# An attention and MLP kernel ordered anew: planner costs and deadlines refitted, four more blocks of exponentials on VectorE, one gelu over w1, U doubled

## The chip, the cores and the metric

The kernel runs on one core of a Trainium2 chip. The metric is the device time of one execution in microseconds (us). "Before" and "changed" are compared on the same chip in the same rounds; only in the first comparison were three of the four runs of "before" taken earlier, before the prediction. A ratio here is the mean time of one kernel's fast runs over that of the other's fast runs in those rounds, with a 95% interval; it is not quite the ratio of the medians that are quoted. All times quoted are of fast runs; one run of the kernel before, of 1394.7 us, was a slow outlier (granted TensorE clock 0.562, against 0.986 to 0.993 in the other runs of its set) and is in no ratio.

## The reference

```python
x = A_x                                         # 2048 tokens, width 640, bf16
xn = layernorm(x)
s = attention(xn, A_wqkv, A_wo)                 # 32 heads of 20, softmax over 2048 keys
g = silu(B(xn))                                 # B below
return x + s * g

def B(x):                                       # shifts(.) moves quarters of the columns by -2..2 tokens
    h  = gelu(layernorm(x) @ w1)
    x1 = x + shifts(h) @ w2
    return x1 + gelu(layernorm(x1) @ w3) @ w4
```

The softmax alone has 32 x 2048 x 2048 exponentials. ScalarE makes most of them, and they fill 789.5 of the 913.2 us of the profile before.

## The kernel before

The program writes a list of tasks, each for one engine with an assumed duration. A planner in the kernel simulates the engines when the program is built and fixes the order of every engine's queue from that simulation. That order then stands: an instruction whose semaphore is not there yet holds up everything behind it in its queue. (In the run `flat_offsets` below, ScalarE waited 8.5 us for value products that stood behind 140 background matmuls on PE.)

Exponentials are made in two ways. On ScalarE one activation takes a 128x1024 score tile (two PSUM banks, two heads). In a "block unit" (`score_both`) the scores of all four heads of a key tile are computed at once: two heads go to ScalarE and two to VectorE, which converts them to 16-bit integers in `U` (L1401) and scales them four times into `SS` (L1308). The scaled bits, read as bf16, are pieces whose weighted sum on PE approximates the exponential. `ND` says how many such blocks each group of queries has. A block covers two key tiles and spares ScalarE two activations.

```python
SYNC_LAT = 130.0                       # one latency for every engine pair, ns
def c_dve(n, kind="psum"):             # assumed VectorE durations
    if kind == "psum" or kind == "1x": return 185 + 1.042 * n
    if kind == "4x":                   return 185 + 0.2605 * n
...
self.LAG = 3;  self.AHEAD = 4          # one lag for all of VectorE's block work
self.ND = ([1,2,3,3], [3,3,3,3], ..., [3,3,3,3], [3,3,2,1])     # 90 blocks
...
pl.pool("W", 3); pl.pool("S", 2)       # banks 5..7 for background, 2 pairs for scores, bank 4 for values
...
# score_both: two heads to S for ScalarE, two to a pair of W banks for VectorE
T("pe", 220, fn, ..., acq=[("S", hs), ("W", h0, h1)])
slot = self.exp_act(hs, sa)            # ScalarE
T("dve", c_dve(1024), fnu, ..., due=cfg.T0 + (self.nact + cfg.LAG) * cfg.STEP)
```

Everything else (projections, both MLP layers, the output projection) is background work for PE and VectorE, placed between scores. It uses the three W banks, which block units use as well.

Of the kernel before, what the change touches and what calls it, by code (L numbers as in the profile page):

```python
# [86 lines left out]
SYNC_LAT = 130.0  # L87
# [40 lines left out]
class Planner:  # L128
    def __init__(self):
# [19 lines left out]
        self.mode_cost = 100.0  # L149
        self.reserve = 0.0  # L150

    def pool(self, name, nslots):
        self.pools[name] = nslots

# [115 lines left out]

    def schedule(self, verbose=False):
# [13 lines left out]
        for t in reversed(tasks):  # L285
            d = t.due if t.due is not None else INF
            for (sid, sync) in t.succs:
                s = tasks[sid]
                sd = s.prio - s.dur - (SYNC_LAT if sync else 0.0) - t.lat
                if sd < d:  # L290
                    d = sd
            if d == INF:
                d = horizon + 1e6
            t.prio = d
# [24 lines left out]
        while done < n:  # L319
            best = None  # L320
            for e in ENGINES:
# [6 lines left out]
                early = None  # L328
                k = 0
                saved = set()  # L330
                while h and k < WINDOW:
# [5 lines left out]
                    if t.acq:  # L337
# [3 lines left out]
                        short = None  # L341
                        for a in t.acq:
                            ft = sorted(x[0] for x in pstate[a[0]])[len(a) - 2]
                            if ft > rt:
                                rt = ft
                            if len(a) > 2 and ft > tf:
                                short = a[0]
                        if short is not None and rt < INF and r0 <= tf + self.reserve:
                            saved.add(short)
# [31 lines left out]
            for pname, *handles in t.acq:  # L381
                ps = pstate[pname]
                idle = [i for i in range(len(ps)) if ps[i][0] <= st + 1e-9]
                mid = (len(ps) - 1) / 2
                if len(handles) == 2:
                    pick = min(((i, j) for i in idle for j in idle if i < j), key=lambda x: (x[1] - x[0], ps[x[0]][0] + ps[x[1]][0]))
                elif pname == "W":
                    pick = (max(idle, key=lambda i: (abs(i - mid), -ps[i][0])),)
                else:
                    pick = (min(idle, key=lambda i: ps[i][0]),)  # L390
                for si, handle in zip(pick, handles):
                    ft, rel_tid = ps[si]
                    handle.slot = si
                    held[id(handle)] = (pname, si)
                    ps[si] = (INF, None)
                    if rel_tid is not None:
                        t.preds.add(rel_tid)
                        tasks[rel_tid].succs.append((t.id, True))
# [14 lines left out]
            for rh in (t.rel if isinstance(t.rel, (list, tuple)) else () if t.rel is None else (t.rel,)):  # L413
                pname, si = held.pop(id(rh))
                pstate[pname][si] = (t.finish + t.lat + SYNC_LAT, t.id)
            for (sid, sync) in t.succs:
# [3 lines left out]
                rt = t.finish + t.lat + (SYNC_LAT if sync else 0.0)  # L420
# [164 lines left out]
class Cfg:  # L585
# [5 lines left out]
    def __init__(self, S=2048, D=640, H=32, F=1536):  # L591
# [12 lines left out]
        self.STEP = 960.0  # L604
        self.BLK = [(2, 3), (6, 7), (10, 11), (14, 15)]
        self.LAG = 3
        self.AHEAD = 4
        self.UNITS = ((), ((3, 0, 1),), ((0, 0, 2), (2, 1, 2)), ((0, 0, 2), (2, 1, 2), (6, 0, 1)),
                      ((0, 0, 2), (1, 1, 2), (4, 0, 2), (5, 1, 2)))
        self.HPS = 6  # L610
        self.EARLY = 15570.0
        self.WO = 20580.0
        self.B1 = (0.64, 0.7)
        self.B2 = (3.06, 0.95)
        self.LEAD = 65220.0
        self.LEAD0 = 56120.0
        self.VLEAD = 9440.0
        self.ND = (
            [1, 2, 3, 3],
            [3, 3, 3, 3],  # L620
            [3, 3, 3, 3],
            [3, 3, 3, 3],
            [3, 3, 3, 3],
            [3, 3, 3, 3],
            [3, 3, 3, 3],
            [3, 3, 2, 1])
# [28 lines left out]
def c_dve(n, kind="psum"):  # L655
    if kind == "psum" or kind == "1x":
        return 185 + 1.042 * n
    if kind == "2x":
        return 185 + 0.521 * n
    if kind == "4x":  # L660
        return 185 + 0.2605 * n
    if kind == "recip":
        return 150 + 6.25 * n
# [3 lines left out]
def c_act(n):  # L667
    return 90 + 0.8333 * n


def c_pe(ninstr, N):
    return ninstr * max(29.0, 0.107 * N)
# [9 lines left out]
class Gen:  # L682
# [50 lines left out]
    def wbank(self, h, dtype=FP32):  # L733
        return self.bank(self.W0 + h.slot, dtype)
# [19 lines left out]
    def build(self, plan_only=False):  # L754
        nc, pl = self.nc, self.pl
        with contextlib.ExitStack() as es:
# [8 lines left out]
            self.W0 = 5  # L765
            pl.pool("W", 3)
            pl.pool("S", 2)
# [14 lines left out]
    def program(self):  # L782
# [15 lines left out]
        for quad in range(cfg.NQUAD):  # L798
# [3 lines left out]
            if quad + 1 < cfg.NQUAD:  # L802
                self.fetch(quad + 1)
            if quad == 1:
                self.v_load(1)
                self.v_proj(1)
            self.run_b(quad)
# [3 lines left out]
        self.T("sp", 10, None, reads=self.out_atoms, name="join", due=cfg.T0 + self.nact * cfg.STEP + 8000.0)  # L811
# [8 lines left out]
    def setup_consts(self):  # L820
# [20 lines left out]
        T("dve", 200, lambda e: e.tensor_reduce(eaug[:, :], e4[:, :], axis=AX.X, op=ALU.add),  # L841
          reads=[A("e4")], writes=[A("eaug")], name="eaug")
        maskh = self.maskh = self.alloc("maskh", [1], FP32)
        T("dve", 200, lambda e: e.tensor_reduce(maskh[:, :], maskn[:, :], axis=AX.X, op=ALU.add), reads=[A("maskn")], writes=[A("maskh")],
          name="maskh0")
        T("dve", 200, lambda e: e.tensor_scalar(maskh[:, :], maskh[:, :], 0.0, None, op0=ALU.is_lt),
# [12 lines left out]
    def alloc_persistent(self):  # L859
# [15 lines left out]
        T("dve", 100, lambda e: e.tensor_tensor(self.maskq[:, :], self.maskh[:, :], self.eaug[:, :], op=ALU.add),  # L875
          reads=[A("maskh"), A("eaug")], writes=[A("maskq")], name="maskq")
        T("dve", 100, lambda e: e.tensor_scalar(self.qbias[:, :], self.eaug[:, :], cfg.OFFSET / cfg.scale, None, op0=ALU.mult),
# [4 lines left out]
        self.U = self.alloc("U", [4096], U16)  # L882
        self.SS = self.alloc("SS", [4, 4096], U16)
# [13 lines left out]
        self.PVB = 4  # L897
# [883 lines left out]
```

## Time and profile before

The first median was 915.4 us (3 runs); together with the run measured beside the changed kernel it is 913.87 us (4 runs).

The profiled run took 914.91 us and its span, from the first to the last instruction, is 913.2 us. ScalarE is the engine to account for: span = its busy time + its idle time. The prediction below works this account out. Two lines of ScalarE's order in time that it does not show matter later. They give start, duration, instruction and, in brackets, the idle time before it and who ended it:

```profile
23.22 2.55 ACT L986 ACTIVATE arena<-arena 128x640 bf16<-128x640 bf16 x3 [5.12 <-DVE arena L982]
...
39.54 21.45 ACT L1369 ACTIVATE arena<-psum 128x1024 bf16<-128x1024 f32 x23 [0.48 <-PE psum L1327]
```

The first is an activation of the opening layer norm that waited 5.1 us for a small VectorE result. The second is the first exponential.

### The profile page before, as it was taken

To read this page: it belongs to the slowest core of one execution; us is meant where nothing else is said; L and a number is where in the kernel's file an instruction comes from. 1 tells how busy PE (TensorE), PEld (TensorE's weight loads), DVE (VectorE), ACT (ScalarE), POOL (GpSimd) and SP (SyncE) were. 2 spreads that over 40 slices of the span, in tenths; PEclk is the share of its full clock that TensorE was granted. 3 is DMA by queue.
4 is the path that set the end of the run, shared out by engine and by line. 5 is a ranking of instruction groups with operands and counts; after the bars stand their busy time and mean duration, and the time that the engine had idled before them with its cause. 6 is when DMAs were issued, how large, how long until landed. Compare 5 with 4: busy or idle time off the path is not lost.

```text
span 913.2 us, 34227 instructions
## 1 busy us (share of the span) xinstructions
PE 838.0 (92%) x15654; PEld 367.2 (40%) x15654; DVE 714.5 (78%) x999; ACT 863.2 (95%) x911; POOL 37.8 (4%) x69
## 2 busy tenths in 40 slices
PE   3899999999999999999998999999997999889996
PEld 1434333444334334433333545433443535324453
DVE  7657788888898889977878778777887667768855
ACT  5898999999999999999999999899999989999995
POOL 7300000000000000100000000000000000100000
PEclk9999999999999999999999999999999999999998
DMA  7003221020122003122123212321122020311322
GB/s 234 11 8 102 77 53 39 25 73 21 36 82 64 19 19 88 31 60 57 43 52 94 72 42 63 89 66 47 45 68 74 18 73 24 99 48 37 108 68 74
DMA packets 83548, 54.81 MB, mean 60 GB/s; under 512 B 52556, under 2 KB 77340, under 8 KB 83276
## 3 DMA queue, kind: packets, MB, share of 16 engines
q1 hardware_dynamic: 83404, 52.62, 20.6%
q8 instruction: 123, 2.02, 0.9%
q14 instruction: 21, 0.17, 0.1%
HBM read 37.91 MB, written 10.63 MB: 53 GB/s over the span
## 4 chain that ended last, share of the span: by engine, by line
ACT 56%; PE 34%; DVE 6%; DMA 3%; issue 1%; SPq 0%; ACTq 0%
ACT arena L1369 51%; PE psum L747 13%; PE psum L1345 11%; PE psum L1286 4%; PE psum L1327 3%; PE psum L1319 2%; DMA arena<-recips 2%; DVE arena L1401 2%; ACT arena L1723 1%; ACT arena L1670 1%; DMA recips<-arena 1%; DVE arena L1308 1%; ACT arena L986 1%; DMA arena<-in_A_x_dram 1%; ACT arena L1739 1%
## 5 line engine op out<-in xcount | busy, mean ns | idle before, releaser
L1369 ACT ACTIVATE arena<-psum 128x1024 bf16<-128x1024 f32 x844 | 789.5, 1034 | 25.4 <-PE psum L1327 16.1
L1345 PE MATMUL psum<-arena 128*32 128x512 bf16 x5088 | 388.7, 382 | 19.3 <-ACT arena L1369 15.1
L747 PE MATMUL psum<-arena 128*32 128x320 bf16 (+1 forms) x5952 | 360.7, 335 | 12.3 <-DVE arena L1124 5.3
L1401 DVE TENSOR_SCALAR arena<-psum 128x1024 uint16<-128x1024 f32 x177 | 216.1, 1221 | 83.3 <-PE psum L1327 82.0
L1308 DVE TENSOR_SCALAR arena<-arena 128x2048 uint16<-128x2048 uint16 (+1 forms) x240 | 219.2, 956 | 2.2 <-PE psum L1319 1.7
L747 PEld LDWEIGHTS psum<-arena 128*32 128x32 bf16 x5952 | 153.3, 97 | 153.5 <-issue 21.6
L1345 PEld LDWEIGHTS psum<-arena 128*32 128x32 bf16 x5088 | 108.5, 95 | 162.6 <-ACT arena L1369 125.6
L1286 PE MATMUL psum<-arena 128*22 128x512 bf16 x1688 | 163.7, 381 | 1.7 <-ACT arena L1369 1.4
L1319 PE MATMUL psum<-arena 128*22 128x512 bf16 x1440 | 115.0, 380 | 2.6 <-DVE arena L1308 2.5
L1327 PE MATMUL psum<-arena 32*128 32x512 bf16 x776 | 82.0, 387 | 14.1 <-DVE arena L1401 5.7
L1286 PEld LDWEIGHTS psum<-arena 128*22 128x22 bf16 x1688 | 43.1, 92 | 58.1 <-issue 13.4
L1327 PEld LDWEIGHTS psum<-arena 32*128 32x128 bf16 x776 | 20.9, 91 | 92.6 <-ACT arena L1369 59.0
L1319 PEld LDWEIGHTS psum<-arena 128*22 128x22 bf16 x1440 | 35.2, 92 | 43.1 <-DVE arena L1308 6.8
L1719 DVE CAST arena<-psum 128x512 bf16<-128x512 f32 x48 | 32.9, 687 | 7.7 <-PE psum L747 7.4
L1170 DVE CAST arena<-psum 128x512 bf16<-128x512 f32 x40 | 27.3, 687 | 9.1 <-PE psum L747 9.0
L1523 DVE SCALAR_TENSOR_TENSOR arena<-psum,arena 128x320 bf16<-128x320 f32 x32 | 15.6, 488 | 17.7 <-PE psum L747 17.2
L1452 DVE TENSOR_TENSOR arena<-arena 128x512 bf16<-128x512 f32 x28 | 19.2, 685 | 9.6 <-DMA arena<-recips 9.6
L935 DVE BATCH_NORM_STATS2 arena<-arena 128x6 f32<-128x320 bf16 x52 | 23.8, 482 | 3.5 <-DMA arena<-in_A_x_dram 3.5
L1734 DVE TENSOR_TENSOR arena<-psum,arena 128x320 bf16<-128x320 f32 x32 | 15.6, 487 | 13.1 <-PE psum L747 12.8
L1034 PE MATMUL psum<-arena 128*32 128x128 bf16 x320 | 8.5, 243 | 16.3 <-DVE arena L949 14.8
L1231 DVE CAST arena<-psum 128x320 bf16<-128x320 f32 x32 | 15.4, 487 | 9.8 <-PE psum L747 9.4
L1723 ACT ACTIVATE arena<-arena 128x12288 bf16<-128x12288 bf16 x2 | 20.9, 10446 | 0.0
(102 smaller groups left out, 295.1 us busy)
## 6 DMA issues: line engine op xcount, KB each, us to landing
arena<-in_B_w_dram SPq DMA_DIRECT2D x48, 160.0 KB, 2.5
arena<-recips SPq DMA_DIRECT2D x28, 256.0 KB
arena<-arena SPq DMA_DIRECT2D x124, 32.0 KB, 1.8
arena<-in_B_w_dram SPq DMA_DIRECT2D x4, 960.0 KB, 5.5
arena<-in_A_x_dram SPq DMA_DIRECT2D x8, 320.0 KB, 5.4
arena<-in_A_x_dram SPq DMA_DIRECT2D x16, 160.0 KB, 3.0
out_dram<-arena SPq DMA_DIRECT2D x16, 160.0 KB, 1.8
arena<-keys SPq DMA_DIRECT2D x28, 80.0 KB
```

The source lines that it names most:

```text
L747: ins = e.matmul(pb[32 * c:32 * c + 32, 0:N], lhsT(k, c), rhs(k, c), start=(k == 0), stop=(stop and k == nk - 1), tile_position=(0, 32 * c))
L935: lambda e, li=li, n=n, hh=hh: e.bn_stats(st[:, li, 6 * hh:6 * hh + 6], xn[:, n, hD * hh:hD * hh + hD]),
L1170: T("dve", c_dve(512), lambda e, h=h, c=c: e.tensor_copy(KS[:, 512 * c:512 * c + 512], self.wbank(h)[:, 0:512]), reads=[wa], writes=[A("KS ...
L1286: ins = e.matmul(pb[32 * i:32 * i + 22, 0:512], VA[:, ql, kts[i // 2], i, :], PT[:, slots[i // 2][0].slot, 512 * (i % 2):512 * (i % 2) + 512],
L1308: T("dve", c_dve(w, "4x"), lambda e, v=v, dst=dst: e.tensor_scalar(dst, U[:, 0:w], 0.5, EXP_B[v], op0=ALU.mult, op1=ALU.add), reads=halves ...
L1319: ins = e.matmul(pb[32 * i:32 * i + 22, 0:512], wv, dst[:, at:at + 512].bitcast(BF16), start=first, stop=final, tile_position=(0, 32 * i))
L1327: return e.matmul(out, self.KT[32 * i:32 * i + 32, b, 128 * kt:128 * kt + 128], self.QT[32 * i:32 * i + 32, b, 512 * qc:512 * qc + 512], s ...
L1345: ins = e.matmul(out[32 * c:32 * c + 32, :], self.KT[:, b, 128 * kt + 32 * c:128 * kt + 32 * c + 32], self.QM[:, gb, 2 * a + jj, :], start ...
L1369: lambda e: e.activation(self.PT[:, hp.slot, :], self.psum[:, 1024 * hs.slot:1024 * hs.slot + 1024], AF.Exp, scale=cfg.scale),
L1401: return e.tensor_scalar(dst, self.psum[:, 512 * (self.W0 + lo):512 * (self.W0 + hi + 1)], a_exp, EXP_BIAS, op0=ALU.mult, op1=ALU.add)
L1719: T("dve", c_dve(512), lambda e, h=h, fc=fc, i=i: e.tensor_copy(GT[:, i, fc, :], self.wbank(h)[:, 0:512]), reads=[wa], writes=at, name=f"g ...
L1723: T("act", 2600 + c_act(2 * FC * 512), lambda e: e.activation(GT[:, :, :, :], GT[:, :, :, :], AF.Gelu_apprx_tanh), reads=gta, writes=gta, ...
```

## The change

What it is meant to do, as the diff reads: give the planner the durations and latencies as measured on the chip, so that its order holds there; refit all deadlines on it; use the room that VectorE then has. The core of the diff, shortened (`...` marks what is left out):

```diff
-SYNC_LAT = 130.0
+SYNC_LAT = {"pe": 225.0, "act": 158.0, "dve": 136.0, "pool": 160.0, "sp": 60.0}
 def c_dve(n, kind="psum"):
-        return 185 + 1.042 * n            # and 185 + 0.2605 * n for "4x"
+        return 72 + 1.042 * n             # and  68 + 0.2605 * n
 def c_act(n):
-    return 90 + 0.8333 * n
+    return 68 + 0.8333 * n
...
-        self.LAG = 3                      # with LEAD, LEAD0, VLEAD, EARLY, WO, B1, B2
-        self.AHEAD = 4
+        self.DUE = dict(k0=-37.9, k1=-9.1, ..., u0=4.0, s0=28.5, u1=7.6, s1=12.5, u2=39.8, s2=57.4,
+            u3=-14.3, s3=3.0, u4=34.6, s4=0.5, u5=59.4, s5=-9.6, u6=-9.6, s6=31.8, u7=-13.7, s7=18.1)
+        self.SAVE = 1; self.THIRD = False; self.FALL = False; self.AHEAD = 3
-            [1, 2, 3, 3], ... [3, 3, 2, 1])
+            [2, 2, 3, 3], ... [3, 3, 3, 4], [3, 3, 3, 3], [3, 3, 4, 3], [4, 2, 3, 2])
...
-            pl.pool("W", 3); pl.pool("S", 2)
+            pl.pool("B", 7)               # "SD": a score pair and a pair of W banks, taken as one
+            pl.kind("SD", "B", [(r + q, x + y) for r, x in pairs for q, y in high])
+            if self.cfg.SAVE: pl.saves = {"SD": "W"}     # hold W tiles back when an SD is short
...
-        self.U = self.alloc("U", [4096], U16);  self.SS = self.alloc("SS", [4, 4096], U16)
+        self.U = self.alloc("U", [2, 4096], U16);  self.SS = self.alloc("SS", [3, 4096], U16)
...
-        self.hx = self.alloc("hx", [2, KC, 512], BF16)      # gelu over w1 in two halves
+        self.hx = self.alloc("hx", [4, KC, 512], BF16)      # one gelu over all of it
-          name=f"u{quad}_{qc}_{kt}", due=cfg.T0 + (self.nact + cfg.LAG) * cfg.STEP)
+          name=f"u{quad}_{qc}_{kt}", due=self.at(self.nact, f"u{quad}"))
```

Offsets in `DUE` are counted in ScalarE steps of 0.96 us. `u0` to `u7` and `s0` to `s7` shift the deadlines of the conversions and scalings of one quad (four heads). Also changed, and not shown here: durations that were written as plain numbers (small VectorE operations are planned at 90 ns in place of 100 to 260), the places of the blocks within a group of queries (`UNITS`), and the priority of VectorE's drain of the value bank, which now goes before background work.

## The prediction

> **What bounds the kernel now.** I read the share of busy time first, then the granted clock (0.992 over the span, so no throttled state), then the chain that ended last, then every wait of ScalarE, then ScalarE's instructions in order of time, and last what PE and VectorE did around the long waits.
>
> ```profile
> PE 838.0 (92%) x15654; PEld 367.2 (40%) x15654; DVE 714.5 (78%) x999; ACT 863.2 (95%) x911; POOL 37.8 (4%) x69
> ...
> ACT 56%; PE 34%; DVE 6%; DMA 3%; issue 1%; SPq 0%; ACTq 0%
> ...
> L1369 ACT ACTIVATE arena<-psum 128x1024 bf16<-128x1024 f32 x844 | 789.5, 1034 | 25.4 <-PE psum L1327 16.1
> ```
>
> ScalarE is busy 863.2 of 913.2 us and heads the chain. Nearly all of it is 844 exponentials, 789.5 / 844 = 0.935 us each back to back. PE shows 92%, but its ends are modelled and it also waits for ScalarE 353 times before column scores (125.6 us at its weight loads), so much of that is pacing by ScalarE. The span is therefore ScalarE's busy time plus its 50.0 us of idle. Where the idle is, ScalarE's waits tell:
>
> ```profile
> ACT arena L1369 <- PE psum L1327: 16.1, 15, 3.5
> ACT arena L1369 <- PE psum L1286: 5.4, 2, 4.1
> ACT arena L986 <- DVE arena L982: 5.1, 1, 5.1
> ACT arena L966 <- DMA arena<-in_A_x_dram: 3.0, 2, 1.7
> ACT arena L1369 <- PE psum L1345: 2.8, 7, 0.8
> ```
>
> The three L1369 rows are the listed waits of the exponentials (24.3 of the 25.4 us that the group shows). The last exponential ends at 902.5 us, so 913.2 - 902.5 = 10.7 us is the tail. The rest, 50.0 - 25.4 - 10.7 = 13.9 us, is start-up before the first exponential at 39.5 us. L1327 is the row-tiled score of a block unit: it makes one tile for ScalarE and one for VectorE, and needs banks from the pool that projections and the MLP also use. Around the longest such wait (start, duration, instruction, idle before it) the timeline has:
>
> ```profile
> 577.53 1.49 DVE L1742 SCALAR_TENSOR_TENSOR arena<-arena 128x1280 bf16<-128x1280 bf16 x1 [1.09 <-ACT arena L1739]
> ...
> 579.34 0.69 DVE L1308 TENSOR_SCALAR arena<-arena 128x2048 uint16<-128x2048 uint16 x1
> 579.48 1.48 PEld L747 LDWEIGHTS psum<-arena 128*32 128x32 bf16 x48 [1.14 <-DVE arena L1734]
> ...
> 580.06 1.22 DVE L1401 TENSOR_SCALAR arena<-psum 128x1024 uint16<-128x1024 f32 x1
> ...
> 581.44 0.40 PE L1327 MATMUL psum<-arena 32*128 32x512 bf16 x4
> ...
> 581.89 1.02 ACT L1369 ACTIVATE arena<-psum 128x1024 bf16<-128x1024 f32 x1 [3.48 <-PE psum L1327]
> ```
>
> VectorE was waiting in order for a tanh; then it drained a background bank, PE used that release for 48 background matmuls, the VectorE score tile was drained only at 581.3, and only then could the next score pair start. Nothing was saturated: the order of the queues was bad. The 4.06 us wait at 77.4 us has the same form: 28 background matmuls stood on PE's queue in front of the three value products that had to release the probability buffers.
>
> **What the Trainium skill says.** *Perfetto Trace Analysis*, § Identifying the Most-Contended Engine, warns that matmul occupancy does not measure PE's nearness to its roof and takes occupancy as fair for ScalarE; the trace agrees (PE "busy" includes its waits). Its § Optimization Strategy says a repeated gap on the engine that should be saturated can mean too little PSUM or SBUF for the next tile: the L1327 rows are of that kind. *ScalarE: Activation LUTs*, § What ACT_TABLE_LOAD costs, gives about 1283 ns for a load plus about 1380 ns of drain, and 186 + 0.833 N ns less about 93 ns of overlap for a back-to-back activation. The trace has the load (1283 ns) but not the drain as a gap: the exponentials end at 176.70, the load starts at 176.71 and the gelu at 178.01. For N=1024 the formula gives 946 ns, the trace 935; I use the trace. *TensorEngine Tiling (Array Packing)*, § Key Properties, says that changing the tiling mode drains PE; after row-tiled groups the trace has a repeated 0.23 us put down to "issue".
>
> **The change part by part.** The operations are nearly unchanged; mostly their order is.
>
> *More blocks on VectorE.* The table of blocks sums to 90 before (9 + 6x12 + 9) and 94 after (10+12+11+12+13+12+13+11). Each block takes two exponentials off ScalarE: 32x32 - 2x90 = 844 becomes 1024 - 188 = 836. On the path: 8 x 0.935 = -7.5 us. VectorE gets, per block, two 128x1024 conversions at 1.22 us and half of four 128x4096 scalings at 1.225 us: 2.44 + 2.45 = 4.9 us, times 4 = +20 us, to about 734 us or 82% of a shorter span. That lies beside ScalarE's work as long as it comes in time. PE loses two column-tiled scores of two heads each (four of about 0.22 us per key tile, eight per block) and gains two row-tiled scores and four pieces, less one value product: about 1.76 + 0.44 against 0.44 + 0.22 + 0.88, so 0.66 us less per block, -3 us, less two more mode changes at about 0.23 us each way. Neutral.
>
> *One gelu over w1.* Two gelus of 5120 elements become one of 10240. Removed are two table loads, 2 x 1.28 = 2.6 us, and one instruction's fixed cost, under 0.2 us. On the path: -2.7 us. In exchange exponentials are interrupted once for about 1.3 + 8.6 + 1.3 = 11.2 us, instead of twice for 7. PE must have background work for that long. The larger gelus are gaps of 13 us already, so this is known territory.
>
> *PSUM pool.* The new kinds look like a shared pool of seven banks, but the switches for a third score pair and for falling back are off. So scores still have two pairs and background three banks, with a pair of those three for VectorE. What is new is that all four banks of a block's score are taken as one, and background tiles are held back when any of the four is short. That aims at the L1327 waits; by itself it creates no room.
>
> *U doubled, SS from 4 to 3 slots.* The conversion into U need no longer wait for the four scalings of the block before it (up to 4 x 1.13 = 4.5 us); three rotating slots are enough as each scaling is 1.13 us apart. This lets L1401 drain PSUM sooner, hence L1327 start sooner.
>
> *Costs and latencies in the planner.* Old: 185 + 1.042 N for VectorE from PSUM, 650 + 67 = 718 ns at N=512; the trace's record is 687 ns and its back-to-back spacing is shorter still (three 128x4096 scalings in 3.49 us are 1.13 apart, while the old model says 1.25 and the new one 1.135). Over 999 instructions the old plan thought VectorE some 115 us busier than it is, and its delay from PE is raised from 130 to 225 ns. Queues in order that were planned on wrong times wait at the wrong places. All deadlines are also refitted and the drain of the value bank is put first. I cannot read the new order off the diff, so what it recovers of the 25.4 us is a judgement: I take 14 us off (11 left), because the long waits shown above are ordering faults and VectorE and PE have unused time in every stretch, but the short ones of 0.3 to 1 us mostly stay: tight coupling with two score pairs. Start-up may win 0.6 us of the wait for L982, which stood behind projection drains in VectorE's queue. The tail is the same instructions.
>
> Sum: 913.2 - 7.5 - 2.7 - 14.4 - 0.6 = 888.0 us of span. The timed runs are about 2 us over the span (915.4 against 913.2): 890.
>
> **Rivals.** (1) *The idle only moves.* VectorE at 82% and PE still near its pace make new waits of the L1401/L1327 kind, and the longer gelu leaves PE without scores. For it: VectorE waits 82 us for L1327 already, and four more blocks add row-tiled changes. Against: it is 5% more work on an engine with 22% idle. Only the 10.2 us of ScalarE's work would be gained: about 905. (2) *The plan is nearly exact.* Then listed waits fall to 3 or 4 us, start-up gains 2 to 3: 880 to 882. For it: ScalarE runs 88 and 106 exponentials with no gap where the order suits it. Against: memory transfers, whose landing the plan only estimates, also gate the order. (3) *VectorE becomes the bound where heavy units meet.* Quads with 13 blocks (rows 5 and 7) share VectorE with MLP drains; a few exponential gaps of 1 to 4 us each there would make 895 to 900.
>
> **Range and chances.** ScalarE's saving of 10.2 us is nearly certain, so slower needs over 28 us of new idle: 0.02. Faster by over 2% means under 897.1, that is, 8.1 us of idle recovered out of 39 that are not tail. I put that at 0.73, and within 2% at 0.25. The range is 880 (rival 2) to 903 (near rival 1).
>
> **What would show it.** Right: 836 exponentials at about 0.935 us; six table loads after the first in place of eight, with one gelu of 128x10240 over w1; ScalarE busy near 853; the idle before exponentials near 11 us with no wait over 2 us; VectorE near 734. Wrong: listed idle of exponentials at 20 us or more, a wait after the long gelu, or VectorE's pieces (L1308's successors) as the releaser of score tiles; a start-up or tail that differs by over 2 us.

## The result and the profile after

The changed kernel took 890.77 us (median of 4 runs, 887.93 to 892.25) against 913.87; ratio 0.974, interval 0.9697 to 0.9783. That is faster by 2.6%.

First the page of the changed kernel: the engines' busy times, the chain that ended last by engine, and the group of the exponentials (busy and mean ns, then idle before them). Line numbers have moved: L1404 was L1369 (exponential), L1362 was L1327 (row-tiled score), L1319 was L1286 (value product), L1380 was L1345 (column-tiled score).

```profile
PE 829.2 (93%) x15630; PEld 364.1 (41%) x15630; DVE 724.4 (81%) x1000; ACT 851.0 (96%) x900; POOL 37.8 (4%) x69
...
ACT 45%; PE 27%; DVE 19%; DMA 8%; issue 1%; SPq 0%
...
L1404 ACT ACTIVATE arena<-psum 128x1024 bf16<-128x1024 f32 x836 | 779.9, 1036 | 16.5 <-PE psum L1362 5.6
```

Then ScalarE's four largest waits: total, number, longest.

```profile
ACT arena L1404 <- PE psum L1362: 5.6, 10, 1.3
ACT arena L1404 <- PE psum L1319: 5.1, 6, 1.6
ACT arena L1001 <- DMA arena<-in_A_x_dram: 4.3, 2, 2.7
ACT arena L1404 <- PE psum L1380: 4.2, 10, 1.0
```

The waits for row-tiled scores fell from 16.1 us in 15 waits, the longest 3.5, to 5.6 us in 10, the longest 1.3. The 5.1 us wait of the layer norm for VectorE is gone. The waits for value products did not shrink (5.4 us in 2 became 5.1 in 6), and those for column scores grew (2.8 to 4.2). In the chain that ended last, ScalarE's share fell from 56 to 45% and VectorE's rose from 6 to 19%. These shares are coarse: in two later profiles of the same changed kernel ScalarE has 38 and 44%.

Next ScalarE's order in time at the start-up, the gelu over w1 and after it:

```profile
16.20 2.54 ACT L1021 ACTIVATE arena<-arena 128x640 bf16<-128x640 bf16 x3
...
36.26 75.28 ACT L1404 ACTIVATE arena<-psum 128x1024 bf16<-128x1024 f32 x81 [0.48 <-PE psum L1362]
...
202.10 1.28 ACT L1698 ACT_TABLE_LOAD   x1
203.39 8.74 ACT L1698 ACTIVATE arena<-arena 128x10240 bf16<-128x10240 bf16 x1
212.15 1.28 ACT L1404 ACT_TABLE_LOAD   x1
213.44 131.06 ACT L1404 ACTIVATE arena<-psum 128x1024 bf16<-128x1024 f32 x141
```

The layer norm's activations start 7 us earlier than before (16.20 against 23.22), the first exponential 3.3 us earlier. There is one gelu of 8.74 us with one table load on each side. After it 141 exponentials run without a listed wait: (131.06 - 1.036) / 140 = 0.929 us each.

What is left looks like this. The lines are PE, VectorE and ScalarE around the longest wait of the changed kernel:

```profile
490.67 0.39 PE L1354 MATMUL psum<-arena 128*22 128x512 bf16 x4
490.94 0.48 DVE L1767 TENSOR_TENSOR arena<-psum,arena 128x320 bf16<-128x320 f32 x1
...
491.33 0.68 DVE L1466 COPY arena<-psum 128x512 f32<-128x512 f32 x1
491.45 0.85 PE L771 MATMUL psum<-arena 128*32 128x320 bf16 x20
...
492.13 0.60 PE L1319 MATMUL psum<-arena 128*22 128x512 bf16 x8
...
492.57 1.02 ACT L1404 ACTIVATE arena<-psum 128x1024 bf16<-128x1024 f32 x1 [1.61 <-PE psum L1319]
```

A group of queries ends with the last piece on PE (490.67). VectorE is then in a background drain, copies the value bank out (491.33), and only then may PE start the next group's value products (492.13), which release the probability buffers that the exponential at 492.57 needs. There is one value bank, so each of the 32 groups needs this turn. All six waits of exponentials for value products (5.1 us) follow such a drain (two of them by a transpose in place of the copy), and so do two waits that are put down to row-tiled scores (0.58 us at 143.75 and 0.56 at 193.30). The other group ends show no wait of that kind.

The trace shows one more thing, which concerns the clock. The mean granted TensorE clock of this profile is 0.992, but that is not an even value: it is 1.00 except from 476.4 to 479.8 us, from 705.1 to 708.5 us and in the tail, where it is 0.50. In the first stretch eight score matmuls take 1.08 us (476.81) that take 0.60 us elsewhere. Five waits of exponentials, 2.9 of the 16.5 us, fall in these two stretches or just after them. Both come shortly after one of the two 10.4 us gelus of the second MLP layer. Before the first, PE was busy for only 1.8 us between 472 and 476 us. In the kernel before, three such stretches before the tail hold 1.5 us of its waits.

The accounts, in us of the profiled runs:

| | before | changed | difference | predicted |
|---|---|---|---|---|
| ScalarE busy | 863.2 | 851.0 | -12.2 | -10.2 |
| idle before exponentials | 25.4 | 16.5 | -8.9 | -14.4 |
| start-up idle | 13.9 | 10.6 | -3.3 | -0.6 |
| after the last exponential | 10.7 | 11.3 | +0.6 | 0 |
| span | 913.2 | 889.4 | -23.8 | -25.2 |

Start-up idle is the rest: 889.4 - 851.0 - 16.5 - 11.3 = 10.6, with the last exponential ending at 857.70 + 20.40 = 878.10.

### The profile page after: what moved, and what is told of

It is laid out like the page before. It is cut to its first block, busy times and chain, and to the rows that moved or that the text cites. A ratio compares the mean times of both kernels' runs of the same rounds, so it can differ in the third digit from the quotient of the medians.

```text
span 889.4 us, 34152 instructions
## 1 busy us (share of the span) xinstructions
PE 829.2 (93%) x15630; PEld 364.1 (41%) x15630; DVE 724.4 (81%) x1000; ACT 851.0 (96%) x900; POOL 37.8 (4%) x69
## 4 chain that ended last, share of the span: by engine, by line
ACT 45%; PE 27%; DVE 19%; DMA 8%; issue 1%; SPq 0%
ACT arena L1404 42%; PE psum L771 11%; PE psum L1380 8%; DVE arena L1345 4%; DVE arena L1431 4%; DMA arena<-recips 4%; PE psum L1362 3%; PE psum L1319 3%; PE psum L1354 2%; DMA recips<-arena 2%; DVE arena L970 2%; DMA queries<-arena 1%; ACT arena L1756 1%; ACT arena L1698 1%; DVE arena L1682 1%
## 5 line engine op out<-in xcount | busy, mean ns | idle before, releaser
L1404 ACT ACTIVATE arena<-psum 128x1024 bf16<-128x1024 f32 x836 | 779.9, 1036 | 16.5 <-PE psum L1362 5.6
L1380 PE MATMUL psum<-arena 128*32 128x512 bf16 x4992 | 380.0, 381 | 11.5 <-ACT arena L1404 9.5
L1431 DVE TENSOR_SCALAR arena<-psum 128x1024 uint16<-128x1024 f32 x188 | 229.1, 1218 | 52.9 <-PE psum L1362 51.8
L1345 DVE TENSOR_SCALAR arena<-arena 128x4096 uint16<-128x4096 uint16 (+1 forms) x236 | 230.1, 1008 | 5.4 <-PE psum L1354 4.1
L771 PEld LDWEIGHTS psum<-arena 128*32 128x32 bf16 x5952 | 147.9, 97 | 148.0 <-issue 27.4
L1380 PEld LDWEIGHTS psum<-arena 128*32 128x32 bf16 x4992 | 106.8, 95 | 145.6 <-ACT arena L1404 102.6
L1319 PE MATMUL psum<-arena 128*22 128x512 bf16 x1672 | 161.6, 381 | 2.0 <-DVE arena L1466 1.7
L1354 PE MATMUL psum<-arena 128*22 128x512 bf16 x1504 | 123.3, 380 | 2.1 <-DVE arena L1345 1.9
L1362 PE MATMUL psum<-arena 32*128 32x512 bf16 x800 | 83.7, 386 | 14.3 <-ACT arena L1404 6.6
L1319 PEld LDWEIGHTS psum<-arena 128*22 128x22 bf16 x1672 | 42.4, 92 | 54.2 <-issue 7.5
L1362 PEld LDWEIGHTS psum<-arena 32*128 32x128 bf16 x800 | 21.4, 91 | 98.8 <-ACT arena L1404 81.7
L1354 PEld LDWEIGHTS psum<-arena 128*22 128x22 bf16 x1504 | 36.4, 92 | 45.5 <-DVE arena L1345 10.6
L1479 DVE TENSOR_TENSOR arena<-arena 128x512 bf16<-128x512 f32 x28 | 19.3, 689 | 16.1 <-DMA arena<-recips 15.8
L1466 DVE COPY arena<-psum 128x512 f32<-128x512 f32 x28 | 19.2, 687 | 3.6 <-PE psum L1354 2.8
L1069 PE MATMUL psum<-arena 128*32 128x128 bf16 x320 | 9.3, 246 | 12.2 <-DVE arena L984 11.8
```

What stands on the lines that cost most here:

```text
L771: ins = e.matmul(pb[32 * c:32 * c + 32, 0:N], lhsT(k, c), rhs(k, c), start=(k == 0), stop=(stop and k == nk - 1), tile_position=(0, 32 * c))
L1319: ins = e.matmul(pb[32 * i:32 * i + 22, 0:512], VA[:, ql, kts[i // 2], i, :], PT[:, slots[i // 2][0].slot, 512 * (i % 2):512 * (i % 2) + 512],
L1345: T("dve", c_dve(w, "4x"), lambda e, v=v, dst=dst: e.tensor_scalar(dst, U[:, ub, 0:w], 0.5, EXP_B[v], op0=ALU.mult, op1=ALU.add), reads=ha ...
L1354: ins = e.matmul(pb[32 * i:32 * i + 22, 0:512], wv, dst[:, at:at + 512].bitcast(BF16), start=first, stop=final, tile_position=(0, 32 * i))
L1362: return e.matmul(out, self.KT[32 * i:32 * i + 32, b, 128 * kt:128 * kt + 128], self.QT[32 * i:32 * i + 32, b, 512 * qc:512 * qc + 512], s ...
L1380: ins = e.matmul(out[32 * c:32 * c + 32, :], self.KT[:, b, 128 * kt + 32 * c:128 * kt + 32 * c + 32], self.QM[:, gb, 2 * a + jj, :], start ...
```

## The experiments

My theory was that ScalarE's work falls by arithmetic and that the idle falls because the order is better, for which true costs and refitted deadlines are both needed. The rivals were that the deadlines alone do it, that costs alone do it, or that the second U or the reservation made room.

There is a trap in undoing one part: any part that is put back also makes the fitted deadlines stale. So in runs called "refit" I fitted the deadlines again, by a random local search over `DUE` judged by the kernel's own planner. Each had four searches of some 1,000 to 1,200 trials, `refit_only` four of some 1,800, and the best of the four was run. As a control, four such searches (some 5,300 trials) found nothing better for the changed kernel itself. (The searches and their counts are not on record; the deadlines that came of them are.) By the planner its own fit is thus stronger than mine. On the chip this handicap does not show in the idle: `nd90_refit`, `two_gelus_refit`, `single_u_refit` and `refit_only` have 13.1 to 13.8 us before exponentials, the changed kernel 16.5 to 20.7. The refitted values that differ from the changed kernel's follow, for whoever wants to rebuild a run; the text below does not need them:

```
nd90_refit:           k0=-47.44, k1=27.21, k2=-57.78, k3=-88.5, k4=-69.75, v0=-8.8, v0s=-0.4, v1=750.09, v1s=42.29, w1=448.55, w1s=-11.49, g1=105.73, x1=295.76, x1s=-5.86, wo=-7.07, st=428.51, g3_0=616.24, g3_2=584.78, si_0=416.41, si_2=707.18, sis=8.52, u0=24.7, s0=25.25, u1=132.53, s1=26.17, u2=30.73, s2=27.5, u3=-6.95, s3=-2.7, u4=184.21, s4=0.54, u5=4.95, s5=200.3, u6=-26.32, s6=-7.78, u7=-40.85, s7=8.52
two_gelus_refit:      k0=-28.01, k1=-34.05, k2=-57.84, k3=-86.28, k4=121.06, v1=863.15, v1s=-2.42, w1=683.61, w1s=-17.53, g1=159.22, x1=255.58, x1s=-6.15, wo=3.59, st=196.86, g3_0=660.8, g3_2=598.26, si_0=415.11, si_2=711.56, sis=8.1, u0=301.85, s0=169.55, u1=42.61, s1=-0.11, u2=-0.43, s2=189.02, u3=-23.08, s3=-2.13, u4=146.94, s4=0.54, u5=200.54, s5=-12.4, u6=-2.31, s6=22.75, u7=-12.85, s7=18.91
single_u_refit:       k0=-26.85, k1=-8.3, k2=-57.39, k3=-76.97, k4=144.64, v1=754.79, v1s=-10.07, w1=386.3, w1s=-10.59, g1=117.88, x1=274.95, x1s=-6.04, wo=1.76, st=183.22, g3_0=540.62, g3_2=628.4, si_0=415.96, si_2=710.63, sis=8.06, u0=5.81, s0=123.53, u1=187.66, s1=31.27, u2=190.41, s2=154.02, u3=-8.16, s3=53.38, u4=42.36, s4=19.74, u5=39.3, s5=22.08, u6=-23.43, s6=117.31, s7=94.06
old_costs_refit:      k0=82.02, k1=12.14, k2=-57.63, k3=-98.9, k4=176.45, v0=-14.25, v0s=-0.59, v1=812.87, v1s=-18.17, w1=552.72, w1s=-15.33, g1=159.4, x1=284.01, x1s=-6.1, wo=2.5, st=200.41, g3_0=432.79, g3_2=647.28, si_0=417.06, si_2=713.67, sis=9.48, u0=3.81, s0=78.7, u1=80.84, s1=244.42, u2=41.52, s2=126.45, u3=-19.59, s3=21.07, u4=30.82, s4=-1.71, u5=62.05, s5=23.47, u6=-7.29, s6=187.66, u7=-9.36, s7=142.48
refit_only:           k0=-34.5, k1=-117.95, k2=-56.82, k3=-96.95, k4=35.56, v0s=5.8, v1=1097.4, v1s=15.71, w1=745.08, w1s=-26.16, g1=182.37, x1=289.44, x1s=-13.7, wo=80.85, st=292.33, g3_0=676.39, g3_2=592.19, si_0=418.17, si_2=719.49, sis=6.99, u0=0.56, s0=270.53, u1=-16.4, s1=185.04, u2=-3.67, s2=297.4, u3=-10.74, s3=315.59, u4=150.82, s4=93.97, u5=214.93, s5=-8.28, u6=-28.5, s6=36.83, u7=12.99, s7=20.85
no_reservation_refit: k0=-38.21, k1=-40.27, k2=-3.84, k3=-39.23, k4=-243.35, v0=20.02, v0s=-1.01, v1=612.8, v1s=28.02, w1=498.88, w1s=-19.5, g1=145.13, x1=309.15, x1s=0.08, wo=-15.63, st=309.52, g3_0=613.41, g3_2=631.6, si_0=491.32, si_2=897.54, sis=3.18, u0=16.01, s0=20.72, u1=144.68, s1=48.38, u2=-55.01, s2=40.67, u3=-146.13, s3=-70.35, u4=158.98, s4=-23.75, u5=-19.07, s5=197.6, u6=-31.86, s6=-15.42, u7=-24.84, s7=40.72
more_blocks_99:       k0=-83.11, k1=-77.84, k2=-126.45, k3=-82.92, k4=-95.01, v0=-12.89, v0s=-0.88, v1=755.19, v1s=42.14, w1=449.73, w1s=40.99, g1=85.89, x1=222.45, x1s=-2.82, wo=11.25, st=310.33, g3_0=821.55, g3_2=537.42, si_0=422.58, si_2=839, sis=5.8, u0=164.2, s0=239.66, u1=754.79, s1=17.49, u2=371.14, s2=18.59, u3=-2.3, s3=4.86, u4=433.92, s4=0.58, u5=-1.96, s5=195.31, u6=-19.43, s6=231.32, u7=-4.52, s7=729.91
```

All twelve gave correct results. The accounts of their profiles, beside the medians and ratios of the timed runs (the first four share one chip's runs of before, median 916.2; the next four 914.39; the last four 915.05):

| run | ScalarE busy | idle before exps | first exp at | tail | span | median (range) | ratio to before |
|---|---|---|---|---|---|---|---|
| flat_offsets | 849.6 | 31.3 | 35.8 | 16.0 | 908.2 | 910.88 (909.98 to 912.87) | 0.9944 |
| nd90_refit | 857.0 | 13.7 | 39.0 | 10.9 | 895.0 | 896.76 (896.22 to 897.81) | 0.9791 |
| two_gelus_refit | 852.7 | 13.1 | 36.8 | 12.2 | 889.1 | 890.73 (889.82 to 891.36) | 0.9723 |
| single_u_refit | 848.7 | 13.8 | 35.4 | 13.6 | 889.6 | 894.76 (891.32 to 899.17) | 0.9784 |
| after_again | 851.9 | 20.7 | 36.0 | 11.3 | 894.2 | 891.28 (886.43 to 895.99) | 0.9742 |
| old_costs_refit | 852.0 | 25.2 | 39.9 | 12.9 | 907.7 | 907.84 (903.58 to 909.4) | 0.9916 |
| before_true_costs | 860.6 | 44.9 | 40.8 | 10.9 | 931.8 | 934.12 (932.75 to 936.44) | 1.0216 |
| before_94_blocks | 857.9 | 56.1 | 38.8 | 11.1 | 940.4 | 938.47 (937.2 to 942.1) | 1.0265 |
| refit_only | 858.9 | 13.8 | 35.7 | 13.5 | 897.1 | 898.82 (897.78 to 900.2) | 0.983 |
| no_reservation_refit | 853.9 | 27.9 | 37.8 | 11.3 | 909.1 | 910.72 (908.21 to 912.98) | 0.9955 |
| more_blocks_99 | 847.3 | 14.6 | 38.4 | 11.6 | 887.2 | 889.06 (887.52 to 891.11) | 0.9726 |
| after_5_rounds | 851.2 | 17.4 | 35.5 | 11.3 | 889.6 | 895.44 (890.06 to 896.22) | 0.9776 |

The tail is the span less the end of the last exponential. A profile is of one run, and not always of a middle one: that of `single_u_refit` is its fastest (891.32 us), that of `after_again` its slowest (895.99 us). Every run counts as fast; clocks of 0.980 to 0.997 occur.

**The changed kernel again, twice.** No edit.

> The changed kernel unchanged, as the yardstick on the chip of these runs. Expected ratio to the kernel before 0.974, as first measured; 888 to 894 us.

> The changed kernel unchanged, on the chip of the run with 99 blocks, to compare the two there. Expected 888 to 894 us, ratio 0.974.

The intervals are 0.9697 to 0.9787 and 0.9751 to 0.9801. The first was as expected; in the second the ratio was a little higher and the median 895.44 lay just above the range given. The same order of instructions ran from 886.4 to 896.2 us, and in its three profiles the idle before exponentials was 16.5, 20.7 and 17.4 us. Part of what varies is the granted clock, and the time goes with it: of the 14 runs of the changed kernel the five with a mean clock of 0.988 to 0.991 took 893.3 to 896.2 us, the five with 0.994 or 0.995 took 886.4 to 892.3 us. The stretches at 0.50 lie in other places in each profile (at 476 and 705 us in the first, at 196 and 701 in `after_again`, at 471 alone in `after_5_rounds`), so the planned order alone does not decide where they fall. Which of the two, clock or waits, comes first is not shown, and only 1.4 of the 20.7 us and none of the 17.4 us of idle lie in these stretches. The size of the gain is therefore 2.2 to 2.6%, and differences of under some 4 us between variants are not to be read from single medians.

**Flat offsets.** The deadlines of VectorE's block work back to a single lag:

```diff
-            u0=4.0, s0=28.5, u1=7.6, s1=12.5, u2=39.8, s2=57.4, u3=-14.3, s3=3.0, u4=34.6, s4=0.5, u5=59.4, s5=-9.6,
-            u6=-9.6, s6=31.8, u7=-13.7, s7=18.1)
+            u0=3, s0=3, u1=3, s1=3, u2=3, s2=3, u3=3, s3=3, u4=3, s4=3, u5=3, s5=3, u6=3, s6=3, u7=3, s7=3)
```

> The changed kernel with one thing undone: the sixteen fitted offsets for when VectorE converts and scales a block (u0..u7, s0..s7, from -14 to +59 steps) all set to 3, the single lag that the kernel before had; costs, blocks, gelu, buffers and reservation stay. If the fitted deadlines carry the recovered idle: the same ScalarE work (about 851 us busy, 836 exponentials), idle before exponentials back to 25 to 40 us, start-up the same, time 903 to 918. If the correct costs, the reservation or the doubled U carry it, the time stays within 888 to 896 with idle near 16.

The work on ScalarE is the changed kernel's, and the time is nearly that of before: setting sixteen numbers of a planner to one value costs 15 to 19 us (0.9944 against 0.974 to 0.9776, of 915). The other deadlines were not fitted again here, so a part of this can be the trap named above; what the sixteen are worth after a new fit is not shown. The time, idle and start-up are inside what the theory gave. The waits for value products grew from 5.1 to 20.8 us, and the timeline around the longest shows how (first the wait's row: total, number, longest; then start, duration, instruction):

```profile
ACT arena L1401 <- PE psum L1316: 20.8, 6, 8.5
...
526.10 6.13 PE L768 MATMUL psum<-arena 128*32 128x320 bf16 x140
...
532.05 0.60 PE L1351 MATMUL psum<-arena 128*22 128x512 bf16 x8
...
532.88 0.68 DVE L1463 COPY arena<-psum 128x512 f32<-128x512 f32 x1
...
533.62 0.83 PE L1316 MATMUL psum<-arena 128*22 128x512 bf16 x12 [0.96 <-DVE arena L1463]
534.07 1.94 ACT L1401 ACTIVATE arena<-psum 128x1024 bf16<-128x1024 f32 x2 [8.52 <-PE psum L1316]
```

On PE's queue 140 background matmuls (6.1 us) stand before the last pieces of a group (532.05). Only after these can VectorE drain the value bank and PE go on with the value products, so ScalarE waits 8.5 us. PE was busy all the time, with work that ScalarE was not waiting for.

**Old costs, refitted.** The planner's cost functions and latencies of before, deadlines searched on that plan (the durations written as plain numbers stay new):

```diff
-SYNC_LAT = {"pe": 225.0, "act": 158.0, "dve": 136.0, "pool": 160.0, "sp": 60.0}
+SYNC_LAT = {"pe": 130.0, "act": 130.0, "dve": 130.0, "pool": 130.0, "sp": 130.0}
-        return 72 + 1.042 * n
+        return 185 + 1.042 * n            # likewise "2x", "4x", "recip", c_act and c_pe
```

> The changed kernel planned on the old costs and the flat 130 ns latency, deadlines fitted again by the same search but judged by that wrong plan. If the true times in the plan matter beyond the fit: idle before exponentials 22 to 32 us and a later first exponential (38 us or more), time 898 to 908. If only the search for deadlines matters (rival), idle 14 to 18, time 889 to 894.

The interval is 0.9887 to 0.9946. Idle, first exponential and time lie where the theory had them.

```profile
ACT arena L1401 <- PE psum L1316: 14.1, 10, 2.9
```

A search on a wrong plan found an order that was 16.6 us worse on the chip than the changed kernel beside it (907.84 against 891.28), though work and buffers were the same; the largest wait is again that for value products. That my search is weaker than the fit of the changed kernel does not explain this: with the same budget on true costs, and with the blocks, the gelus or `U` put back, it came to 890.7 to 896.8 us. The profile has a stretch of 10.2 us at clock 0.50 from 44.4 us on, with 3.1 of its 25.2 us of idle.

**True costs alone, on the kernel before.**

```diff
 # in the kernel before
-SYNC_LAT = 130.0
+SYNC_LAT = {"pe": 225.0, "act": 158.0, "dve": 136.0, "pool": 160.0, "sp": 60.0}
-def c_dve / c_act / c_pe of before
+def c_dve / c_act / c_pe of the change
```

> The kernel before with only the planner's costs and latencies replaced by the new ones: 90 blocks, two gelus, single U, deadlines as they were. ScalarE busy stays near 863. If true costs alone give a better order: idle before exponentials 10 to 18, time 898 to 908. If true costs without refitted deadlines are worth nothing (my theory after the run with flat offsets): idle 25 to 45, time 912 to 930.

```profile
ACT arena L1369 <- PE psum L1327: 36.0, 20, 5.7
ACT arena L986 <- DVE arena L982: 5.9, 1, 5.9
ACT arena L1369 <- PE psum L1345: 5.5, 10, 1.5
```

Again only the cost functions and latencies were replaced; durations written as plain numbers stayed old. This made it slower by 2.2% (interval 1.019 to 1.0243). The waits for row-tiled scores more than doubled, from 16.1 to 36.0 us. The idle was at the upper end of what the theory expected and the time 4 us above it. The old deadlines belong to the old plan, and here a truer plan with deadlines that were not fitted to it is worse than the wrong plan with its own.

**Four more blocks alone, on the kernel before.**

```diff
 # in the kernel before
-            [1, 2, 3, 3], [3, 3, 3, 3], ..., [3, 3, 2, 1])
+            [2, 2, 3, 3], [3, 3, 3, 3], [3, 3, 3, 2], [3, 3, 3, 3], [3, 3, 3, 4], [3, 3, 3, 3], [3, 3, 4, 3], [4, 2, 3, 2])
```

> The kernel before with only the table of blocks of the changed kernel (94). ScalarE busy falls by 7.5 us to about 856. If the blocks are worth their ScalarE time in any order: 906 to 910. If the order of before, planned on too slow a VectorE, cannot take them: idle before exponentials 35 to 60, time 915 to 945.

```profile
ACT arena L1369 <- PE psum L1327: 32.3, 30, 3.2
ACT arena L1369 <- PE psum L1286: 11.4, 5, 5.7
ACT arena L1369 <- PE psum L1345: 11.3, 16, 2.3
```

ScalarE's busy time fell by 5.3 us and its idle before exponentials rose by 30.7, so the kernel was slower by 2.6% (interval 1.0238 to 1.0291). Each kind of wait grew. Six stretches at clock 0.50 before the tail hold 7.2 us of the idle, against 1.5 in the kernel before, so the clock is a part of this but not most of it. Part of the change, taken alone, does the opposite of its purpose.

**The order alone.** The changed kernel with the work of before, and its buffers but for `hx`, which keeps four chunks:

```diff
-            [2, 2, 3, 3], ... [4, 2, 3, 2])              # 94 blocks
+            [1, 2, 3, 3], ... [3, 3, 2, 1])              # 90
-        T("act", 2750 + c_act(4 * KC * 512), ... name="gelu1", ...)
+        for g in (0, 2): T("act", 2750 + c_act(2 * KC * 512), ... hx[:, g:g + 2] ... due=self.at(30.0 * g - 60.0, "g1"))
-        U [2, 4096], SS [3, 4096]; AHEAD = 3
+        U [1, 4096], SS [4, 4096]; AHEAD = 4
```

> The changed kernel with blocks (90), two gelus, single U and four SS slots, and the look-ahead of 4 put back as before, so ScalarE's work is that of the kernel before (about 861 us busy); what stays is planning on the true costs, the joint reservation and deadlines fitted again. If the order alone recovers most of the idle: idle before exponentials 16 to 22, first exponential at 35 to 37 us, time 900 to 906. If the order needs the second U or fewer exponentials to do it (rival): idle 25 or more, time 908 to 916.

```profile
L1400 ACT ACTIVATE arena<-psum 128x1024 bf16<-128x1024 f32 x844 | 785.6, 1042 | 13.8 <-PE psum L1358 6.5 <-PE psum L1376 5.2 <-PE psum L1315 1.4
```

It was better than expected: 898.82 us (interval 0.981 to 0.9849), with only 13.8 us idle. From before to here the profile's span fell by 16.1 us: idle before exponentials -11.6, ScalarE busy -4.3, start-up idle -3.0 (from 13.9 to 897.1 - 858.9 - 13.8 - 13.5 = 10.9), tail +2.8. The order, with true costs, fit and the joint taking of banks, carries most of the gain; the new places of the blocks, the priority of the value bank's drain and the work on w1 done in one go before w2 are in this kernel too, and none of them was tested alone. The same 844 exponentials take 785.6 us instead of 789.5. Records of neighbours overlap (a record is 1.04 us, the spacing 0.93), so a delay of up to about 0.1 us can hide inside "busy". That the better order removes it is not shown: `before_true_costs`, with far more waits, has 786.6 us for its 844.

**90 blocks, refitted.** Only the table of blocks as before.

```diff
-            [2, 2, 3, 3], ... [4, 2, 3, 2])
+            [1, 2, 3, 3], ... [3, 3, 2, 1])
```

> The changed kernel with the table of blocks of before (90 in place of 94, so 844 exponentials), and the deadlines fitted again by a search on the kernel's own planner with the same costs. If four more blocks are worth what ScalarE saves: 8 x 0.933 = 7.5 us more ScalarE work, busy about 858.5, idle as in the changed kernel (14 to 20), time 896 to 901. If the extra load on VectorE costs as much as ScalarE saves, the time stays within 888 to 894 with less idle; if it were only a matter of fit, ScalarE busy would not move with the time.

The time is in the range of the theory (interval 0.9774 to 0.9808). ScalarE is busy 6.0 us longer (8 exponentials more), and the idle is 2.8 us less than in the first profile of the changed kernel. In the ratio the four blocks are worth between 0.15 and 0.5% (0.9791 against 0.974, 0.9742 and 0.9776; the intervals overlap), so at best 5 us of the 7.5. On the same chip, `two_gelus_refit` below has the 94 blocks, one gelu more and a refit like this one, and is 6.0 us faster (890.73 against 896.76). That VectorE's added 20 us of work gives the rest back as waits is not shown: two other refits with 94 blocks idle as little as this one (13.1 and 13.8 us against 13.7).

**Two gelus, refitted.** The edit is that of `refit_only` for the gelu alone.

> The changed kernel with the gelu over w1 split again in two of 128x5120 at different times, deadlines fitted again. Theory: two table loads more (2 x 1.283 us) and one more fixed cost: ScalarE busy plus 2.7 us, idle as before, time plus 2.5 to 5, 893 to 896. Rival, the long gelu starves PE and the split one is smoother: ScalarE busy plus 2.7 but idle falls by as much, time within 1 us of 890.8.

```profile
L1401 ACT ACTIVATE arena<-psum 128x1024 bf16<-128x1024 f32 x836 | 778.8, 1037 | 13.1 <-PE psum L1316 6.0 <-PE psum L1377 3.3 <-PE psum L1359 3.1
...
L1697 ACT ACTIVATE arena<-arena 128x5120 bf16<-128x5120 bf16 x2 | 8.9, 4472 | 0.0
...
L1401 ACT ACT_TABLE_LOAD x4 | 5.1, 1283 | 0.1
```

The rival's numbers came. There are two gelus of 4.47 us and two more table loads (one before the second gelu, one after it). ScalarE is busy 1.7 us longer, the idle is 3.4 us lower (in the changed kernel's first profile 2.9 us of idle lie in stretches at clock 0.50, of which this profile has none before the tail), and the time is that of the changed kernel (interval 0.9707 to 0.974). The merged gelu gains nothing that these runs can show. The rival's cause, that it starves PE, is not what the trace shows: PE is busy for 6.8 of the 7 us from 206 to 213, and no exponential is listed as waiting just after this gelu.

**One U, refitted.**

```diff
-        self.U = self.alloc("U", [2, 4096], U16);  self.SS = self.alloc("SS", [3, 4096], U16)
+        self.U = self.alloc("U", [1, 4096], U16);  self.SS = self.alloc("SS", [4, 4096], U16)
-        ub = self.unit % 2 ... k = self.piece % 3
+        ub = 0 ... k = self.piece % 4
```

> The changed kernel with U single and four SS slots as before, deadlines fitted again. ScalarE work is the same. If the second U lets VectorE drain score tiles sooner: idle before exponentials 19 to 25 instead of 16.5 and a tail 1 to 2 us longer, time 894 to 900, and more of VectorE's conversions waiting for scalings. If U is not what blocks (rival: order alone), the time is 889 to 892.

This is inconclusive. The median, 894.76, is at the lower edge of what the theory of U expected and the tail is 2.3 us longer (1 to 2 were expected), but the idle before exponentials (13.8 us, in the fastest of its four runs) is not higher. No view shows conversions waiting for scalings, which was expected too; both stand in VectorE's own queue. The runs spread over 8 us, and the interval of the ratio (0.9752 to 0.9816) overlaps those of the changed kernel. What the second U is worth is 0 to 0.4%.

**No reservation, refitted.** Background tiles are never held back for a block unit.

```diff
-        self.SAVE = 1
+        self.SAVE = 0
```

> The changed kernel without holding background tiles back when a block's four banks are short, deadlines fitted again as well as the search could. ScalarE busy the same 851. If the reservation is needed: row-tiled scores wait for banks that background tiles keep taking, idle before exponentials 30 to 45, mostly put down to the row-tiled score, time 903 to 917. If the reservation is a detail (the kernel before had a weaker form of it): 888 to 895.

```profile
ACT arena L1401 <- PE psum L1359: 14.0, 12, 5.9
ACT arena L1401 <- PE psum L1316: 9.0, 11, 2.4
ACT arena L1073 <- PE psum L1066: 7.8, 3, 5.4
```

The time (910.72, interval 0.994 to 0.997) is where the theory had it; the idle, 27.9 us, is a little under its range. Row-tiled scores are the largest wait again, the longest 5.9 us. It does not say that the new reservation is better than the one before: the kernel before also held W tiles back when a block lacked W banks. It says that without any the same search ends 15 us above the changed kernel on the same chip (910.72 against 895.44).

**A try at beating both: 99 blocks.** The planned time of an exponential raised to the measured spacing, table of blocks and deadlines searched together (some 10,000 trials in each of four searches, then 9,000 from the best):

```diff
-    return 68 + 0.8333 * n        # c_act
+    return 80 + 0.8333 * n
+            [2,3,3,3], [3,3,4,3], [3,3,3,2], [3,3,2,3], [4,4,3,4], [3,3,3,3], [3,4,4,4], [4,2,3,2])     # ND
```

> A try at beating both: 99 blocks in place of 94 (826 exponentials), the planner's activation cost raised by 12 ns so that an exponential is planned at the measured 0.933 us, deadlines and table of blocks searched together. ScalarE busy 851 - 10 x 0.933 = 842; VectorE up by 5 x 4.9 us to about 749, 85% of the span. If VectorE still has room: idle 17 to 23, time 882 to 888. If VectorE now makes the waits: idle 25 or more, 890 or slower.

```profile
PE 826.3 (93%) x15570; PEld 370.7 (42%) x15570; DVE 744.6 (84%) x1012; ACT 847.3 (96%) x890; POOL 37.9 (4%) x69
...
L1400 ACT ACTIVATE arena<-psum 128x1024 bf16<-128x1024 f32 x826 | 776.2, 1031 | 14.6 <-PE psum L1315 6.9
```

The time is 889.06 us, interval 0.9705 to 0.9748, against 895.44 (0.9751 to 0.9801) of the changed kernel on the same chip. So it beats both there, by half a per cent over the changed kernel and with intervals that do not overlap, but its ratio is no better than the changed kernel's 0.974 elsewhere. It is a tie or a very small gain, and neither expectation came: the idle is below both, the time between them. The saving on ScalarE did not come through: ten exponentials fewer should be 9.3 us, but busy fell by 3.9 us (851.2 to 847.3), because the spacing of an exponential grew to 776.2 / 826 = 0.940 us, and the first exponential came 2.9 us later. VectorE is busy 744.6 us.

## Why the prediction was right or wrong

The time was right: 890 predicted, 890.77 measured, the class as well. Its steps were right in part, and the closeness is luck: against the predicted account ScalarE's work was 2.0 us less, the idle before exponentials 5.5 us more, the start-up 2.7 us less and the tail 0.6 us more, which leaves 1.4 us of span (889.4 for 888.0).

- **What bounds the kernel: right.** Every run above is read as ScalarE busy plus ScalarE idle. The runs with unchanged work show the rest is order: `flat_offsets` has ScalarE's work of the changed kernel and nearly the time of before.
- **ScalarE's work: right in kind, too small by 2 us.** The counts (836 exponentials, three table loads before exponentials in place of four, and seven in all in place of nine) came as said. The exponentials took 779.9 us where 836 x 0.935 = 781.7 was assumed. The step "789.5 / 844 = 0.935 us each back to back" took the mean of all for the undisturbed spacing; a stretch without a listed wait has 0.929.
- **Idle, "I take 14 us off (11 left)": the step that failed.** 8.9 us came off, 16.5 were left (17.4 and 20.7 in the other two profiles). The ordering faults shown there did go: no exponential waits longer than 1.6 us in the first profile (2.0 and 2.5 in the other two). But I had no term for the single value bank, after whose turn the waits for value products still add up to 5.1 us, six in each of the three profiles, nor for stretches at half the clock, which hold 2.9 us of the first profile's idle and less of the others. Refits with true costs and the reservation came to 13.1 to 13.8 us, with 90 blocks as with 94 (14.6 with 99); none came to 11.
- **Start-up, "may win 0.6 us": the term was too small.** It won 3.3 us, so one of the prediction's own signs of being wrong came true ("a start-up or tail that differs by over 2 us"). The layer norm's wait on VectorE (5.1 us) vanished, and other waits took its place only in part.
- **"By itself it creates no room" (PSUM pool): not tested.** No bank was added, as said. Without any reservation the refitted kernel stays at 910.7, but the kernel before held tiles back too; what the new form adds to the old one no run shows.
- **The gelu, "-2.7 us on the path": not confirmed.** Two table loads were saved, as worked out, but the refitted kernel with two gelus is as fast.
- **U: open.** Between nothing and 0.4%.
- **VectorE: the operations right, the engine's sum 10 us too high.** Conversions rose from 216.1 + 3.9 (six that had been split) to 229.1, scalings from 219.2 to 230.1: +20.0 as predicted. The engine's busy time rose only by 9.9, to 724.4. Of the rest, 5.2 us are other records that got shorter, mostly of the layer norm. The last 4.9 us are overlap: the groups' busy times add up to 754.6 and 769.4 us, 40.1 and 45.0 more than the engine's, since records of neighbours overlap.
- **Rivals.** "The idle only moves" is what happens to the parts without the fit (934 and 938 us), and not to the whole. "Nearly exact" was right about the start-up and wrong about the waits. The gaps of rival 3 came, but small: four of 1.0 to 1.6 us in the whole run.
- **Slips that did not reach the sum.** The old cost at N=512 is 185 + 533 = 718 ns, not "650 + 67". VectorE's 20 us more are 2.8% of its 714.5 us, not "5%". PE's busy time, whose ends are modelled, fell by 8.8 us where 3 were worked out. The 2 us between span and time compare two runs; within one run they are 1.7 to 1.8 us (914.91 against 913.2, 891.17 against 889.4).

In one sentence: most of the gain is the refitted order on true costs (before to `refit_only`, 16 us), and the parts that cut ScalarE's work, with the buffers, add some 3 to 8 us on top, from 898.8 to between 890.8 and 895.4 (3.4 us on the same chip).

## What to carry to other kernels

When queues are fixed in advance, durations, latencies, deadlines and the split of work are one fit: changing any of them alone, even towards the truth, can cost about as much as the whole is worth (here 20 and 24 us lost against 23 won). So judge a part by putting it back and fitting the rest again, not by putting it back alone. Look for long waits of the bound engine in which the releaser was busy with work that this engine did not need yet, and at single buffers that must be turned at the end of each group.

## What the Trainium skill lacked or had wrong

- *ScalarE: Activation LUTs*, § What ACT_TABLE_LOAD costs: the drain of about 1.38 us per switch of tables does not appear. In the changed kernel the load at 202.10 lasts 1.28 us and the gelu starts at 203.39; the load back at 212.15 is followed by an exponential at 213.44. A switch cost 1.29 us here. From the section's formula one works out 946 ns for a back-to-back activation of 1024 elements (an estimate); it was 0.929 us where undisturbed (141 in 131.06 us).
- *TensorEngine Tiling (Array Packing)*, § Key Properties, says that a change of the tiling mode drains PE but gives no size: here the weight load after a row-tiled group starts 0.23 us late, put down to "issue" (489.67 us in the changed kernel's timeline; at full clock 82% of 212 such gaps are 0.20 to 0.26 us). That the drain is the cause is not shown.
- *Perfetto Trace Analysis*, § Identifying the Most-Contended Engine, takes ScalarE's occupancy as a fair measure. With overlapping records it can hide delays of up to 0.1 us per instruction (1.04 us of record, 0.93 of spacing): the same 844 exponentials were "busy" 789.5, 786.6, 786.2 and 785.6 us in four orders.
- No page says how much the order of fixed queues can be worth. Here, with the same instructions on ScalarE, it was 19 us of span (908.2 in `flat_offsets` against 889.4).
